# Narrowing in steps, products moved to GpSimd and ones products in the prologue of a two-block kernel

## The chip, the cores and the metric

The kernel runs on one core of one Trainium2 chip. The metric is the device time of one execution in microseconds, as the median over runs. The core has five engines with instruction queues of their own: TensorE (PE in the profile, its weight loads PEld) for matrix products, VectorE (DVE), ScalarE (ACT), GpSimd (POOL) and SyncE (SP), which here only issues transfers. Every queue is worked off in order. An instruction waits on semaphores for what it needs from other engines.

## The reference

Two blocks follow one another. The first is a linear attention over q, k, v of shape (4, 4, 1088, 32) (batch, heads, sequence, head dimension) with two random 8x32 matrices S1, S2 as sketches:

```python
def phi(x):
    a = np.einsum('rd,bhsd->bhsr', S1, x)
    b = np.einsum('rd,bhsd->bhsr', S2, x)
    return np.einsum('bhsi,bhsj->bhsij', a, b).reshape(*x.shape[:-1], r * r)
q_p, k_p = (phi(q), phi(k))
kv = np.einsum('bhsf,bhsd->bhfd', k_p, v)
z = np.sum(k_p, axis=2)
num = np.einsum('bhsf,bhfd->bhsd', q_p, kv)
den = np.einsum('bhsf,bhf->bhs', q_p, z)[..., None] + 1e-06
return (num / den).astype(np.float32)
```

Its result, laid out as x of 4352 tokens by 128, goes through a gated feed-forward block with 1536 hidden units:

```python
gate = 1.0 / (1.0 + np.exp(-(x @ w_gate)))
val = x @ w_val
return (gate * val @ w_out).astype(np.float32)
```

S1, S2 and the three weight matrices arrive as 64-bit floats, everything else as 32-bit floats.

## The kernel before

**The feed-forward block** holds tokens in chunks of 512 columns of `xT` (eight full ones and a half one) and hidden units in 12 blocks of 128. One *wave* (`w1`, L287) is one block for one chunk: the gate and the value product into the two halves of a PSUM tile (`wave`, L300, two products of 512 columns, which the profile counts as four records), the sigmoid on ScalarE (`sg`, L308), and later the product of both on VectorE (`g`, L313, by `glu`). `w2` (L252) adds g times w_out into `moeout` (L258), about two waves later, and after the twelfth block turns and stores the chunk. A *slot* (`slot`, L327) runs one group of attention work and then some waves, each with the `glu` of the wave before and a due `w2` ahead of it. So the attention of later batches is strewn between the waves, in an order that is written out by hand.

**Weights.** `load_w(n)` (L135) loads two blocks of all three matrices as pairs of 32-bit words into `w_in`, which has four buffers. `narrow` (L81) makes 32-bit floats from the halves: cap (L94, VectorE, clamps the upper word as a float), head (L99 and L103, VectorE, shifts and masks), tail (L107, ScalarE, the lower word), a Square of cap (L108, ScalarE), the add of tail to head as integers (L109, GpSimd), and at last the product into `w_sb` (L113, VectorE), which sets tiny values to zero. All but the last run at once in `narrow_w(j)` (L158), and the last in `narrow_last(j)` (L165). In chunk 0, wave j calls `narrow_w(j + 3)` and `narrow_last(j + 1)`; blocks 0, 1 and 2 are narrowed ahead of the first wave.

**Attention.** For a batch: `turn_k` (L351) and `turn_q` (L362) turn k and q on VectorE in blocks of 32; `kps` (L375) projects k with both sketches and turns the result into `kab`; `outer` (L395) makes the 64 features of k for one head as an outer product, on VectorE (L399, `kp`); `kv` (L450) sums features times v on TensorE (L459, `kvz`), and features times ones for z, or, in batches 1 to 3, z from `sum_z` (L489), four adds on VectorE (L493 to L497). `ab` (L406) projects q with the sketches spread over 64 columns (`aps`, `bps`, L422), copies one to SBUF on ScalarE (`asb`, L432) and multiplies on VectorE (`mult`, L441, `qp`). `ndt` (L500) turns the sums on TensorE and copies them on VectorE into `zb` (L514) and `nd` (L516). `den` (L518) gives the denominators, whose `invert` on VectorE (L534 to L541) makes `rb`, and `num` (L551) the numerators, whose `divide` (L568) writes `xT`. Queries go in two parts of 18 and 16 rows of 32 (`q_chk`).

**Order.** SP's queue first holds the loads of S1 and S2, batch 0's k and q, each in two parts, v, the weights 0 to 7 and batch 1. The prologue (L578 to L601) runs batch 0 up to the first part of xT, with the narrowing of blocks 0 and 1 between `kv` and `ndt`, and of block 2 after `divide`. Then come seven slots with one wave each, the loop over batches 1 to 3, in which batch 1 has one wave a slot and the others mostly two, and the remaining waves. PSUM tile `wave` has two buffers, shared by waves, `aps` and some `bps`; the tiles `two` (kps, bps, nps) and `one` (kvz, ndps, dps) have one each.

Of the kernel before, what the change touches and what calls it, by code (L numbers as in the profile page):

```python
# [20 lines left out]
def kernel(  # L21
# [34 lines left out]
    sbN = ctx.enter_context(tc.tile_pool(name="sbN", bufs=4))  # L56
# [17 lines left out]
    q_chk = [(0, 9), (9, TP - 9)]  # L74
# [6 lines left out]
    def narrow(out, bits):  # L81
# [7 lines left out]
        def tmp(dt, tag):  # L89
            return sbN.tile([P, 3, P], dt, tag=tag, name=tag)[:, :n, :m]  # L90


        cap, head, tail = tmp(I32, "cap"), tmp(I32, "head"), tmp(I32, "tail")
        nc.vector.tensor_scalar(  # L94
            out=cap.bitcast(F32), in0=hi.bitcast(F32), scalar1=122880.0, scalar2=-122880.0,
            op0=ALU.min, op1=ALU.max,
        )

        nc.vector.tensor_scalar(  # L99
# [6 lines left out]

        nc.scalar.activation(out=tail, in_=lo, func=ACTF.Copy, scale=2.0**-29)  # L107
        nc.scalar.activation(out=cap.bitcast(F32), in_=cap.bitcast(F32), func=ACTF.Square)  # L108
        nc.gpsimd.tensor_tensor(out=head, in0=head, in1=tail, op=ALU.add)  # L109


        def last():
            nc.vector.scalar_tensor_tensor(  # L113
                out=out, in0=cap.bitcast(F32), scalar=1.265625 * 2.0**-30, in1=head.bitcast(F32),
                op0=ALU.is_ge, op1=MUL,
            )

        return last
# [37 lines left out]
    narrowed = {}  # L156

    def narrow_w(j):  # L158
# [6 lines left out]
    def narrow_last(j):  # L165
        if j in narrowed:
            narrowed.pop(j)()


    def load_rows(src, b, tag, parts=((0, T),)):  # L170
        t = ld.tile([P, T, D], F32, tag=tag, name=tag)
        for t0, t1 in parts:
            nc.sync.dma_start(
# [24 lines left out]
    halves = ((0, T0), (T0, T))  # L198
# [16 lines left out]

    sig0 = const.tile([P, 1], F32, tag="sig0")
    nc.scalar.activation(out=sig0, in_=ones[:, :1], func=ACTF.Sigmoid)
    if wide:
        narrow(sr, sr_in)()
    ident = const.tile([P, P], F32, tag="ident")  # L220
    make_identity(nc, ident)

    hm = const.tile([P, 2, R], F32, tag="hm")
    nc.vector.memset(hm, 0.0)
    for h in range(H):
        nc.vector.memset(hm[32 * h : 32 * h + 32, h % 2, :], 1.0)

# [13 lines left out]

    zb = []
    for n in range(2):
# [43 lines left out]
    def w1():  # L287
# [399 lines left out]
```

## Time and profile before

| | |
|---|---|
| median of 3 runs | 342.51 us (342.16 to 343.34) |
| profiled execution, its own time | 344.44 us |
| its span, first to last instruction | 342.6 us |
| TensorE busy | 314.2 us, 92% |
| VectorE busy | 163.3 us, 48% |
| ScalarE busy | 85.1 us, 25% |
| GpSimd busy | 15.0 us, 4% |
| first wave starts | 24.90 us |

Times of a row are microseconds from the start of the span. A row of a group ends with the idle time of the engine just before these instructions, and what ended it. "x4" counts records; a 32-bit product is two records. TensorE's busy time also counts the slow parts, where the granted clock is half.

### The profile page before, as it was taken

To read this page: it belongs to the slowest core of one execution; us is meant where nothing else is said; L and a number is where in the kernel's file an instruction comes from. 1 tells how busy PE (TensorE), PEld (TensorE's weight loads), DVE (VectorE), ACT (ScalarE), POOL (GpSimd) and SP (SyncE) were. 2 spreads that over 40 slices of the span, in tenths; PEclk is the share of its full clock that TensorE was granted. 3 is DMA by queue.
4 is the path that set the end of the run, shared out by engine and by line. 5 is a ranking of instruction groups with operands and counts; after the bars stand their busy time and mean duration, and the time that the engine had idled before them with its cause. 6 is when DMAs were issued, how large, how long until landed. Compare 5 with 4: busy or idle time off the path is not lost.

```text
span 342.6 us, 3915 instructions
## 1 busy us (share of the span) xinstructions
PE 314.2 (92%) x1552; PEld 137.8 (40%) x1552; DVE 163.3 (48%) x294; ACT 85.1 (25%) x152; POOL 15.0 (4%) x21
## 2 busy tenths in 40 slices
PE   1839878599999999999999999999999999999994
PEld 0512323133334434334443344444444444444682
DVE  3874798965675455475344432233233232322321
ACT  2143442123122222222222122222222222222220
POOL 1032131110000000000000000000000000000000
PEclk9995999989999999999999999999999999999999
DMA  6999302211100001000100010002001000100010
GB/s 166 303 316 310 65 0 68 65 35 36 31 2 1 2 16 17 0 0 2 31 2 0 0 32 2 0 0 32 0 0 25 7 0 0 32 0 0 2 31 15
DMA packets 25586, 14.08 MB, mean 41 GB/s; under 512 B 19168, under 2 KB 22752, under 8 KB 25568
## 3 DMA queue, kind: packets, MB, share of 16 engines
q1 hardware_dynamic: 25568, 13.83, 16.0%
q8 instruction: 12, 0.20, 0.2%
q14 instruction: 6, 0.05, 0.0%
HBM read 11.60 MB, written 2.23 MB: 40 GB/s over the span
## 4 chain that ended last, share of the span: by engine, by line
PE 83%; DVE 10%; DMA 2%; issue 2%; ACT 1%; SPq 1%; DVEq 0%
PE wave L300 49%; PE moeout L258 25%; PE aps L422 3%; PE kvz L459 2%; DMA q<-in_q_dram 2%; DVE g L313 1%; PE dps L523 1%; DVE head L103 1%; DVE cap L94 1%; PE nps L558 1%; DVE w_sb L113 1%; PE bps L422 1%; DVE head L99 1%; DVE kp L399 1%; DVE qT L368 1%
## 5 line engine op out<-in xcount | busy, mean ns | idle before, releaser
L300 PE MATMUL wave<-xT,w_sb 128*128 128x512 f32 (+1 forms) x432 | 195.7, 581 | 6.0 <-DVE w_sb L113 4.8
L313 DVE TENSOR_TENSOR g<-wave,sg 128x512 f32<-128x512 f32 x102 | 69.9, 685 | 122.7 <-ACT sg L308 122.7
L300 PEld LDWEIGHTS wave<-xT,w_sb 128*128 128x128 f32 x432 | 82.3, 193 | 103.4 <-issue 84.1
L308 ACT ACTIVATE sg<-wave 128x512 f32<-128x512 f32 x102 | 60.8, 596 | 204.3 <-PE wave L300 204.3
L258 PE MATMUL moeout<-g,w_sb 128*128 128x512 f32 (+1 forms) x216 | 107.4, 590 | 1.8 <-DVE g L313 1.8
L258 PEld LDWEIGHTS moeout<-g,w_sb 128*128 128x128 f32 x216 | 38.1, 191 | 44.1 <-issue 38.0
L441 DVE TENSOR_TENSOR qp<-bps,asb 128x576 f32<-128x576 f32 (+1 forms) x16 | 11.4, 720 | 22.9 <-PE bps L422 17.9
L422 PE MATMUL aps<-qT,s 32*64 32x288 f32 (+1 forms) x128 | 12.4, 468 | 5.0 <-DVE qT L368 2.8
L109 POOL TENSOR_TENSOR head<-head,tail 128x384 int32<-128x384 int32 (+1 forms) x13 | 14.1, 1089 | 55.3 <-DVE head L103 42.4
L108 ACT ACTIVATE cap<-cap 128x384 f32<-128x384 f32 (+1 forms) x13 | 6.5, 502 | 29.4 <-DVE head L103 29.4
L380 PE MATMUL kps<-kT,sk 64*32 64x288 f32 x64 | 3.9, 482 | 9.6 <-DVE kT L356 9.6
L399 DVE TENSOR_TENSOR kp<-kab 128x576 f32<-128x576 f32 (+2 forms) x20 | 12.5, 665 | 0.0
L422 PE MATMUL bps<-qT,s 32*64 32x288 f32 (+1 forms) x128 | 12.2, 451 | 0.0
L432 ACT COPY asb<-aps 128x576 f32<-128x576 f32 (+1 forms) x16 | 9.8, 610 | 8.0 <-PE aps L422 6.5
L422 PEld LDWEIGHTS aps<-qT,s 32*64 32x64 f32 x128 | 4.0, 147 | 18.2 <-issue 9.1
L568 DVE TENSOR_TENSOR xT<-nps,rb 128x576 f32<-128x576 f32 (+1 forms) x8 | 5.8, 724 | 7.7 <-PE nps L558 7.6
L459 PE MATMUL kvz<-kp,v 128*32 128x64 f32 (+1 forms) x288 | 8.8, 246 | 0.2 <-DVE kp L399 0.2
L459 PEld LDWEIGHTS kvz<-kp,v 128*32 128x32 f32 (+1 forms) x288 | 6.3, 124 | 6.2 <-issue 4.0
L103 DVE SCALAR_TENSOR_TENSOR head<-cap,head 128x384 int32<-128x384 int32 (+1 forms) x13 | 6.9, 533 | 0.5
L368 DVE STREAM_TRANSPOSE qT<-q 128x576 f32<-128x576 f32 (+1 forms) x8 | 5.9, 736 | 1.7 <-DMA q<-in_q_dram 1.7
L268 DVE STREAM_TRANSPOSE o_sb<-moeout 128x512 f32<-128x512 f32 (+1 forms) x9 | 6.1, 676 | 1.2 <-PE moeout L258 1.2
L107 ACT ACTIVATE tail<-w_in 128x384 int32<-128x384 uint32 x12 | 6.6, 553 | 0.0
(46 smaller groups left out, 87.1 us busy)
## 6 DMA issues: line engine op xcount, KB each, us to landing
v<-in_v_dram SPq DMA_DIRECT2D x16, 144.0 KB, 7.6
k<-in_k_dram SPq DMA_DIRECT2D x3, 544.0 KB, 7.0
q<-in_q_dram SPq DMA_DIRECT2D x3, 544.0 KB, 8.5
w_in<-in_moe_w_gate_dram SPq DMA_DIRECT2D x6, 256.0 KB, 5.6
w_in<-in_moe_w_val_dram SPq DMA_DIRECT2D x6, 256.0 KB, 5.6
w_in<-in_moe_w_out_dram SPq DMA_DIRECT2D x6, 256.0 KB, 5.7
out_dram<-o_sb SPq DMA_DIRECT2D x20, 64.0 KB, 2.0
k<-in_k_dram SPq DMA_DIRECT2D x1, 288.0 KB, 2.9
```

The source lines that it names most:

```text
L103: nc.vector.scalar_tensor_tensor(out=head, in0=cap, scalar=-0x40000000, in1=head, op0=ALU.bitwise_and, op1=ALU.bitwise_or)
L109: nc.gpsimd.tensor_tensor(out=head, in0=head, in1=tail, op=ALU.add)
L258: nc.tensor.matmul(out=moe["acc"][:, :tw], lhsT=w_sb[:, 2, j, :], rhs=g[:, jj, :tw], start=(j == 0), stop=(j == NJ - 1),)
L300: nc.tensor.matmul(out=wv[:, which, jj * tw : (jj + 1) * tw], lhsT=w_sb[:, which, j0 + jj, :], rhs=xT[:, t0 : t0 + tw], start=True, stop=True,
L308: nc.scalar.activation(out=sg, in_=wv[:, 0], func=ACTF.Sigmoid)
L313: nc.vector.tensor_tensor(out=g, in0=wv[:, 1], in1=sg, op=MUL)
L368: nc.vector.transpose(out=qT_of[b][:, t0 : t0 + tn].rearrange("p t c s -> p (t c s)"), in_=q_t[b][:, 2 * t0 : 2 * (t0 + tn)].rearrange("p ...
L399: nc.vector.tensor_tensor(out=KP[b][:, h, j0:j1].rearrange("p j (i l) -> p j i l", i=R), in0=bass.AP(tensor=a0.tensor, offset=a0.offset, a ...
L422: nc.tensor.matmul(out=dst[64 * c : 64 * c + 64, m, : 32 * tn], lhsT=sx[rows, :], rhs=qT_of[bb][rows, t0 : t0 + tn, c, :], start=True, sto ...
L432: nc.scalar.copy(out=ASB[a_of][:, :, :w], in_=aps[:, :, :w])
L441: nc.vector.tensor_tensor(out=QP[bb][:, 2 * pr : 2 * pr + 2, 32 * t0 : 32 * t0 + w], in0=bps[:, :, :w], in1=ASB[b_of][:, :, :w], op=MUL,)
L459: nc.tensor.matmul(out=kvz[32 * h : 32 * h + 32, F * which : F * which + F], lhsT=v_t[b][:kr, h, j, :] if which == 0 else ones[:kr, :], rh ...
```

## The change

- **Loads:** the first part of batch 0's k (18 rows of 32) is issued on ScalarE's queue, ahead of all else there; q's first part has 16 rows instead of 18, and its second part is loaded after the first weights.
- **Ones products:** `warm(n)` issues n products of a constant 128x128 view of ones with itself, into a buffer of `wave` that nothing reads: 14 at the start, 4 after `kps(0)`, 4 after the first `ab` groups.
- **Small moves in the prologue:** the constants hm, ident and zb are made before S1 and S2 are narrowed.
- **Narrowing in three steps:** `narrow` becomes a generator. Step 0 is cap, for the weights now on GpSimd, and tail; step 1 is head, Square and add; step 2 the last product. In chunk 0, wave j runs step 0 of block j + 4, step 1 of j + 2 and step 2 of j + 1. Ahead of the first wave stand step 0 of blocks 0 to 3, steps 1 of blocks 0 and 1 and step 2 of block 0.
- **GpSimd:** `outer` runs there for all batches, except for three of four heads in batch 0, and so do the four adds of `sum_z`.
- **ScalarE:** makes the copy into `nd`.
- **Slots:** the prologue's slots become nine, with `turn_k(1)` a slot ahead of `kps(1)`, and `outer` of batch 1 between slots. In the loop, `kv` runs in one slot for all nine steps, later than before; the `ab` groups of a batch follow one another; batch 1 has one wave a slot, the others two.

```diff
-    q_chk = [(0, 9), (9, TP - 9)]
+    q_chk = [(0, 8), (8, TP - 8)]
...
+        cap, tail = tmp(I32, "cap", 5), tmp(I32, "tail", 4)
+        eng.tensor_scalar(
             out=cap.bitcast(F32), in0=hi.bitcast(F32), scalar1=122880.0, scalar2=-122880.0,
             op0=ALU.min, op1=ALU.max,
         )
-
+        nc.scalar.activation(out=tail, in_=lo, func=ACTF.Copy, scale=2.0**-29)
+        yield
+
+        head = tmp(I32, "head", 3)
         nc.vector.tensor_scalar(
...
         nc.gpsimd.tensor_tensor(out=head, in0=head, in1=tail, op=ALU.add)
...
+        yield
+
+        nc.vector.scalar_tensor_tensor(
+            out=out, in0=cap.bitcast(F32), scalar=1.265625 * 2.0**-30, in1=head.bitcast(F32),
+            op0=ALU.is_ge, op1=MUL,
+        )
+        yield
...
+    def narrow_w(j, step):
+        if not 0 <= j < NJ:
+            return
         n, jj = divmod(j, 2)
         if wide:
-            narrowed[j] = narrow(w_sb[:, :, j, :], w_in[n][:, :, jj])
-        if jj == 1 and n + 4 < NJ // 2:
+            if step == 0:
+                narrowing[j] = narrow(w_sb[:, :, j, :], w_in[n][:, :, jj], nc.gpsimd)
+            next(narrowing[j])
+        if step == 0 and jj == 1 and n + 4 < NJ // 2:
             load_w(n + 4)
...
-    k_t[0] = load_rows(k, 0, "k", halves)
-    q_t[0] = load_rows(q, 0, "q", halves)
+    k_t[0] = load_rows(k, 0, "k", ((0, KBASE[2] + 1, nc.scalar), (KBASE[2] + 1, T, nc.sync)))
+    q_t[0] = load_rows(q, 0, "q", ((0, T0, nc.sync),))
     v_t[0] = load_v(0)
-    for n in range(4):
+    load_w(0)
+    load_rows(q, 0, "q", ((T0, T, nc.sync),), q_t[0])
+    for n in range(1, 4):
         load_w(n)
...
+    def warm(n):
+        t = psm.tile([P, 2, 512], F32, tag="wave", name="warm")
+        x = bass.AP(tensor=ones.tensor, offset=ones.offset, ap=[list(ones.ap[0]), [0, P]])
+        for _ in range(n):
+            nc.tensor.matmul(out=t[:, 0, :P], lhsT=x, rhs=x, start=True, stop=True)
+
+    warm(14)
...
-            if j0 + 3 < NJ:
-                narrow_w(j0 + 3)
-            narrow_last(j0 + 1)
+            narrow_w(j0 + 4, 0)
+            narrow_w(j0 + 2, 1)
+            narrow_w(j0 + 1, 2)
...
-    def outer(b, h, j0=0, j1=NJK):
+    def outer(b, h, j0=0, j1=NJK, eng=nc.gpsimd):
...
-        nc.vector.tensor_copy(out=ND[b], in_=ndps[:, 0, :P])
+        nc.scalar.copy(out=ND[b], in_=ndps[:, 0, :P])
...
     kps(0)
+    warm(4)
     ab((0, 0, 0))
     mult00 = ab((0, 1, 0), (0, 0, 0))
     mult10 = ab(None, (0, 1, 0), (psm, "wave"))
-    for h in range(H):
-        outer(0, h, 0, 5)
-    kv(0, [1, 2, 3, 4])
-    for h in range(H):
-        outer(0, h, 5, NJK)
+    warm(4)
+    for j0, j1 in ((0, 5), (5, NJK)):
+        outer(0, 3, j0, j1)
+        for h in range(3):
+            outer(0, h, j0, j1, nc.vector)
+        if j0 == 0:
+            kv(0, [1, 2, 3, 4])
     mult00()
     mult10()
     kv(0, [5, 6, 7, 8, 0])
-    narrow_w(0)
-    narrow_w(1)
+    narrow_w(0, 0)
+    narrow_w(1, 0)
+    narrow_w(0, 1)
     ndt(0)
+    narrow_w(2, 0)
+    narrow_w(3, 0)
     invert = den(0, 0)
     divide = num(0, 0)
     invert()
     divide()
-    narrow_w(2)
-    narrow_last(0)
+    narrow_w(0, 2)
+    narrow_w(1, 1)
     turn_q(0, 1)
...
     slot(lambda: r_group((0, 1, 1), (0, 0, 1)), 1)
-    turn_q(1, 0)
-    slot(lambda: r_group((1, 0, 0), (0, 1, 1)), 1)
+    slot(lambda: r_group(None, (0, 1, 1)), 1)
     slot(lambda: den(0, 1)(), 1)
     slot(lambda: num(0, 1)(), 1)
     turn_k(1)
+    slot(None, 1)
     slot(lambda: kps(1), 1)
+    turn_q(1, 0)
+    outer(1, 0)
+    slot(lambda: r_group((1, 0, 0), None), 1)
+    outer(1, 1)
...
+        slot(lambda: r_group((b, 1, 0), (b, 0, 0)), wn)
         if b == 1:
+            outer(b, 2)
+        turn_q(b, 1)
+        slot(lambda: r_group((b, 0, 1), (b, 1, 0)), wn)
+        if b == 1:
+            outer(b, 3)
+        zs = sum_z(b)
+        slot(lambda: r_group((b, 1, 1), (b, 0, 1)), wn)
+        turn_k(b + 1)
+        slot(lambda: kv(b, [1, 2, 3, 4, 5, 6, 7, 8, 0], zs), wn)
+        if more:
+            slot(lambda: kps(b + 1), wn)
             for h in range(H):
-                outer(b, h)
...
+                outer(b + 1, h)
         turn_q(b + 1, 0)
...
+        slot(lambda: ndt(b), wn)
+        slot(lambda: r_group((b + 1, 0, 0) if more else None, (b, 1, 1)), wn)
+        slot(lambda: den(b, 0)(), wn)
...
-        slot(num0_den1, 1)
-        if more:
-            outer(b + 1, 3)
+        slot(num0_den1, wn)
         slot(lambda: num(b, 1)(), 1)
```

More of the change, by code (lines that the diff above doesn't have):

```diff
@@ L226 @@
         nc.vector.memset(hm[32 * h : 32 * h + 32, h % 2, :], 1.0)
+    ident = const.tile([P, P], F32, tag="ident")
+    make_identity(nc, ident)
+    zb = []
+    for n in range(2):
+        t = const.tile([P, H, 32], F32, tag=f"zb{n}", name=f"zb{n}")
+        nc.gpsimd.memset(t, 0.0)
+        zb.append(t)
+    if wide:
+        for _ in narrow(sr, sr_in, nc.vector):
+            pass
     sk = const.tile([P, 2, 2, R], F32, tag="sk")
@@ L240 @@
     sk = sk.rearrange("p m n r -> p (m n r)")
-    zb = []
-    for n in range(2):
-        t = const.tile([P, H, 32], F32, tag=f"zb{n}", name=f"zb{n}")
-        nc.gpsimd.memset(t, 0.0)
-        zb.append(t)
     xT = const.tile([P, NTOK], F32, tag="xT")
@@ L398, in outer @@
         jn = j1 - j0
-        nc.vector.tensor_tensor(
+        eng.tensor_tensor(
             out=KP[b][:, h, j0:j1].rearrange("p j (i l) -> p j i l", i=R),
@@ L576, in num, with r_group @@
         return divide
-    turn_k(0, halves)
+    def r_group(a_of, b_of):
+        m = ab(a_of, b_of)
+        if m is not None:
+            m()
+    turn_k(0, ((0, KBASE[2] + 1), (KBASE[2] + 1, T)))
     turn_q(0, 0)
     kps(0)
+    warm(4)
     ab((0, 0, 0))
```

69 lines of the change are left out of this document (15 added, 54 removed).

## The prediction

> **What bounds the kernel now.** I read the page's head and its row of granted clock by slices first, then stretches cut where the granted clock changes. Columns of the second fence: stretch, its length, busy time of PE, PEld, DVE, ACT and POOL with instruction counts, granted clock, DMA share, GB/s.
>
> ```profile
> span 342.6 us, 3915 instructions
> PEclk9995999989999999999999999999999999999999
> ```
>
> ```profile
> 20.80:24.20 3.40, 0.05 (x8) 0.00 (x0) 3.16 (x7) 0.00 (x0) 0.00 (x0) 1.00 1.06 274
> ...
> 31.05:34.50 3.45, 3.45 (x12) 1.00 (x18) 0.90 (x2) 0.76 (x2) 1.18 (x1) 0.50 1.02 317
> 34.50:68.60 34.10, 25.56 (x179) 8.93 (x163) 30.80 (x54) 11.31 (x23) 7.09 (x6) 1.00 0.18 49
> 65.20:68.60 3.40, 1.21 (x19) 0.25 (x17) 3.26 (x7) 0.00 (x0) 0.00 (x0) 1.00 0.00 0
> 68.60:72.00 3.40, 3.19 (x8) 1.09 (x5) 3.37 (x7) 1.48 (x3) 1.18 (x1) 0.50 0.00 0
> 80.00:337.00 257.00, 256.49 (x1056) 114.63 (x1054) 103.10 (x171) 59.97 (x101) 0.00 (x0) 1.00 0.05 9
> ```
>
> From 80 us on TensorE does not stop (256.49 of 257 us), and the change takes no product away from it. So only what lies before 80 us can be won. There VectorE is the bound from 34.5 to 68.6 (30.80 of 34.10 us, TensorE idle 8.5), and TensorE has half its clock twice: after it stood still from 20.8 to 24.2, until 34.5, and again after a stretch with 1.21 us of work. VectorE's groups from 24.9 to 72 us (busy us, mean ns):
>
> ```profile
> L313 DVE TENSOR_TENSOR g<-wave,sg 128x512 f32<-128x512 f32 x9 | 6.1, 676 | 2.0 <-ACT sg L308 2.0
> L113 DVE SCALAR_TENSOR_TENSOR w_sb<-cap,head 128x384 f32<-128x384 f32 x10 | 5.5, 552 | 0.0
> L103 DVE SCALAR_TENSOR_TENSOR head<-cap,head 128x384 int32<-128x384 int32 x9 | 5.0, 559 | 0.3
> L94 DVE TENSOR_SCALAR cap<-w_in 128x384 f32<-128x384 f32 x9 | 4.8, 534 | 0.0
> L399 DVE TENSOR_TENSOR kp<-kab 128x576 f32<-128x576 f32 x4 | 3.6, 948 | 0.0
> L99 DVE TENSOR_SCALAR head<-cap 128x384 int32<-128x384 int32 x9 | 3.2, 360 | 0.3
> L441 DVE TENSOR_TENSOR qp<-bps,asb 128x512 f32<-128x512 f32 (+1 forms) x4 | 2.8, 711 | 4.2 <-PE bps L422 3.2 <-PE aps L422 1.0
> L356 DVE STREAM_TRANSPOSE kT<-k 128x1088 f32<-128x1088 f32 x2 | 2.6, 1302 | 0.0
> ```
>
> The change takes the caps (4.8), the outer products (3.6) and batch 1's sums off this list. The way to the first wave, from the timeline (start, length, idle before and its releaser), the key/value products in the chain of waits, and their record means of 0 to 17.4 us and of 100 to 320 us:
>
> ```profile
> 9.32 0.78 DVE L368 STREAM_TRANSPOSE qT<-q 128x576 f32<-128x576 f32 x1 [1.67 <-DMA q<-in_q_dram]
> 10.02 0.81 DVE L390 STREAM_TRANSPOSE kab<-kps 128x288 f32<-128x288 f32 x2
> 10.75 3.00 DVE L399 TENSOR_TENSOR kp<-kab 128x320 f32<-128x320 f32 x8
> 15.27 0.55 DVE L94 TENSOR_SCALAR cap<-w_in 128x384 f32<-128x384 f32 x1 [0.19 <-DMA w_in<-in_moe_w_out_dram]
> 17.69 0.37 ACT L482 COPY kvd<-kvz 128x256 f32<-128x256 f32 x1 [4.54 <-PE kvz L459]
> 18.20 0.41 PE L503 MATMUL ndps<-ident,kvd 128*128 128x128 f32 x2 [0.59 <-ACT kvd L482]
> 19.07 0.29 DVE L516 COPY nd<-ndps 128x128 f32<-128x128 f32 x1
> 20.26 0.48 DVE L534 STREAM_TRANSPOSE dT<-dps 128x288 f32<-128x288 f32 x1 [0.90 <-PE dps L523]
> 22.17 0.76 DVE L568 TENSOR_TENSOR xT<-nps,rb 128x576 f32<-128x576 f32 x1
> 24.90 3.78 PE L300 MATMUL wave<-xT,w_sb 128*128 128x512 f32 x4 [4.05 <-DVE w_sb L113]
> ```
>
> ```profile
> 13.46 4.20 PE kvz L459 x144
> ```
>
> ```profile
> L459 PE MATMUL kvz<-kp,v 128*32 128x64 f32 x64 | 3.4, 314 | 0.0
> ```
>
> ```profile
> L459 PE MATMUL kvz<-kp,v 128*32 128x64 f32 (+1 forms) x144 | 3.1, 223 | 0.0
> ```
>
> A key/value record takes 314 ns early against 223 later: TensorE starts at half clock, though the early clock rows say otherwise. Between xT (22.17 + 0.76) and the first wave (24.90) stand the first three operations of narrowing block 2 and the last of block 0, 1.97 us.
>
> **The change, part by part.** *Prices on GpSimd.* First the lock, in timeline rows and in the minimum, median and maximum of two lines, ns:
>
> ```profile
> 42.96 1.18 POOL L109 TENSOR_TENSOR head<-head,tail 128x384 int32<-128x384 int32 x1 [3.71 <-DVE head L103]
> 43.77 0.41 DVE L536 TENSOR_SCALAR rc<-dT 128x16 f32<-128x16 f32 x1
> ```
>
> ```profile
> L536 DVE TENSOR_SCALAR rc<-dT x8: 172/174/411, 20.8 to 191.1; 128x18 f32<-128x18 f32 x4, 128x16 f32<-128x16 f32 x4
> ```
>
> ```profile
> L493 DVE TENSOR_TENSOR z<-kp x3: 1214/1217/2023, 63.6 to 153.9; 128x1024 f32<-128x1024 f32 x3
> ```
>
> ```profile
> 5.10 0.29 POOL masks.py:199 TENSOR_SCALAR_AFFINE_SELECT ident<-ident 128x128 f32<-128x128 f32 x1
> ...
> 18.60 1.96 POOL L109 TENSOR_TENSOR head<-head,tail 128x384 int32<-128x384 int32 x2 [12.92 <-ACT tail L107]
> ```
>
> L536 needs 174 ns and took 411 at 43.77, ending at 44.18 as GpSimd's add ended at 44.14; L493 needs 1.22 us and took 2.02 at 63.6 beside another add. So some VectorE operations stand still while GpSimd works, and each operation moved there is paid in part by VectorE. The Trainium skill (SBUF — State Buffer, SBUF: two separate sides) says the two share one port pair, held for a whole instruction; the trace agrees by those 0.24 and 0.81 us. Its rule speaks against this change; by it two heads of outer products in parallel cost their sum.
>
> A two-input add of 384 costs 0.98 (1.96 for two), or 1.18 beside VectorE: 2.6 to 3.1 ns an element. An outer product of 576 is then 1.5 to 1.8 us; batch 1's sums (1024, 512, 256 and 256 elements) 5.2 to 6.3. A cap on GpSimd has no row; it has one tensor input: between 0.29 (128 elements, as if all fixed) and 1.18; I take 0.7, three times 0.29 less some fixed part. GpSimd's order is one queue; up to the key/value products of batch 1 it holds 12 caps, 12 adds, 6 outer products and the sums: 8.4 + 14.2 + 8.4 + 5.5 = 36.5 us from about 9.5, so done near 50 to 55, before the 13th wave that needs it (67, below).
>
> *Prologue.* The first part of k goes by ScalarE's queue past the loads of S on SP's, and q's second part moves behind the first weights. That issue stands ahead of ScalarE's table load, for which nothing waits so early. The loads of w4 and w5 wait on SP for the caps and tails that free their buffers; behind them stand only batch 2's, wanted tens of us later. VectorE's wait of 1.67 us for q can go wholly or not at all; I take 1.2: kab at 8.8, outer products from 9.5. Eight on VectorE took 3.00; six are 2.25, the two others 1.7 on GpSimd: together 2.25 if they overlap, 3.95 if they take turns; by the lock rows I take 3.7: done at 13.2. TensorE comes out of its 14 products warm; ten of the eighteen key/value steps are left then, of 4.20 us at half clock, so 10/18 of 2.1 = 1.2: kvd at 14.5 instead of 17.69. Behind it VectorE has the two mult (0.71 each, to 14.6) and now the two head steps of w0 (0.36 + 0.56, 0.3 of lock) ahead of the zb copies; so zb ends near 16.2, where it ended at 19.07, and dT starts at 17.1. dT to the end of xT is 2.67 (20.26 to 22.93); with 0.25 of lock at rc, 20.0 less what full clock saves of den, 0.2. Then only w_sb's product is left, 0.55, where before came 1.97: **first wave at 20.3 instead of 24.9**. Bounds 18.3 (no lock, full 1.67) and 22 (no gain at q; w0 no earlier than its 15.27). nd's copy moves to ScalarE, behind the Square of w0, which waits for these heads too: ready near 16.5, before num asks for it.
>
> *The 22 ones products.* 14 products are 28 records of 128 columns. A 512-wide record streams in 0.43 (1.72 for four, below), so 0.107 at full and 0.215 at half clock: 6.0 us, from about 1 to 7, some 2 us ahead of kab. The transposes, 128 wide, took 0.41 for two with all latency, which would make 5.7, and at half clock 11.5: the upper end. I take 6.0. The two groups of 4 fall into waits for q and the outer products; uncovered they cost at most 0.9 each.
>
> *The clock afterwards.* From num to the first wave TensorE again idles some 3.1 us. The row of 65.20 shows that 1.21 us of work in 3.4 already lost the clock, so half clock comes again. It came back only after a stretch without a pause (31.05 to 34.50): in the new order wave 2 starts 5.5 after wave 1 (below), and a filled stretch ends 3.4 to 6.8 later, near 31. By the Trainium skill (TensorE: Matmul & The Clock Gate, What's actually happening) half clock follows at least one idle window of about 3.4 us; 3.1 us would hold none, the first rival. The trace differs: the stretch of 65.20 was not idle.
>
> *The slots of chunk 0.* From the chain of waits:
>
> ```profile
> 30.44 3.78 PE wave L300 x4
> ...
> 73.41 0.83 PE kvz L459 x40
> ...
> 75.55 1.72 PE wave L300 x4
> 77.88 1.06 PE moeout L258 x2
> 78.94 1.72 PE wave L300 x4
> ```
>
> TensorE needs 1.72 for a wave, half of it (0.86, two records of four) for moeout, and for a group of eight or sixteen products 0.3 to 0.6 (75.55 + 1.72 = 77.27 to 77.88): 2.6 to 3.2 us. VectorE needs 0.68 (g) + 0.36 + 0.56 + 0.55 = 2.15 without the cap, plus the group: den 1.91 (20.26 to 22.17), num and turn_k 0.7 + 1.3, kps 0.81 and turn_q 0.78, the slot with mult and turn_q 0.71 + 0.78. The longer of the two, starting from 20.3: wave 2 at 25.8 (as 24.90 to 30.44), wave 3, after 3.4 for wave 2 and 1.3 and 1.7 for group and moeout at half clock (the last of it at full), at 31.8; then 3.0, 4.2, 4.3, 2.7, 3.9, 3.0, 3.9, 3.4, 3.4: the 12th wave at 63.6. I add 1.2 of lock in the slots that VectorE binds: 64.8, against 78.94. Bounds of this lock: none, and 11 (three waits of 0.3 in each of 12 narrowings).
>
> **Sum.** At the 12th wave the old order had the key/value products (0.83) behind it, the new one not: 78.94 - 64.8 - 0.83 = 13.3 us. Span 342.6 - 13.3 = 329.3. The profiled execution took 344.44 with its launch, its span is 0.1 over the runs' median of 342.51; so the forecast is **329 us**. In the later batches the moved operations cost nothing, since TensorE binds there and VectorE has 154 of 257 us free; uncovered, an outer product late by 1 us costs 1 us only if kv meets it.
>
> **Rivals.**
> - *The clock stays full, or is back after one wave.* For it: the gap is 3.1 us, under the 4.05 of before. Against: the 65.20 row. Waves 2 to 4 come 6 us earlier: 323.
> - *VectorE and GpSimd take turns.* For it: the rows of L536 and L493; GpSimd would be busy over half of the stretch. 7 of the 11 us show, the rest lies in TensorE's half clock: 336.
> - *The prologue does not move.* The ones products hold TensorE until 12.4 (11.5 us), or w0's arrival stays where it was; first wave near 24.9: 334.
> - *Slower than before: GpSimd's queue is late for batch 1's key/value products*, and all waves stand behind these on TensorE. Its 36.5 us may grow by some 15 before anything waits; with operations twice my price it ends at 9.5 + 73 = 82.5, 15.5 past 67: 345. It decides from a factor 1.9 on. Against: the adds' rows.
> - *No effect that shows*: gains and lock cancel, 342.5.
>
> **How the numbers follow.** Forecast 0.50, full clock 0.18, turns 0.17, prologue 0.08, GpSimd late 0.04, no effect 0.03. About 0.3% is what a measurement of this kernel can tell from no change. Faster 0.93, same 0.03, slower 0.04. The forecast's own range, by a first wave at 18.3 to 22 and 0 to 4 us of lock, is 325 to 334; 321 to 337 takes in most of the first three rivals.
>
> **What would show it.** First wave near 20; TensorE's granted clock half from about 20 to 31 and never again; no wait of TensorE for L94's successor; key/value products early at 223 ns a record; GpSimd busy some 55 to 60 us, VectorE some 25 less; L103, L113 or L536 lengthened where GpSimd works; the 12th wave near 65. A first wave after 23, or key/value products of batch 1 waiting for GpSimd, would make me wrong.

## The result and the profile after

The changed kernel takes **333.05 us** (median of four runs, 333.0 to 333.84), beside 342.34 us for the kernel before on the same chip: a ratio of 0.974 with a 95% interval of 0.969 to 0.979. The forecast was 329 with a range of 321 to 337: the time lies inside the range, 4 us above the forecast. The profiled execution took 333.0 us, its span is 331.2, 11.4 less than before; the forecast's span was 329.3. That the span fits to 1.9 us is luck: it comes from two large misses of opposite sign, as the stages show. Some executions have a lower granted clock and take longer; times and ratios here leave these out, but the profile of the kernel with the outer products and sums of batches 1 to 3 back on VectorE is of such an execution.

First the page's head of the changed kernel, then three of its stretches (columns as in the prediction: length, busy time of PE, PEld, DVE, ACT, POOL, granted clock, DMA share, GB/s). Line numbers are those of the changed kernel.

```profile
span 331.2 us, 4024 instructions
PE 313.7 (95%) x1596; PEld 141.8 (43%) x1596; DVE 140.9 (43%) x252; ACT 86.3 (26%) x156; POOL 52.3 (16%) x59
PEclk9967999999999999999999999999999999999998
```

```profile
14.83:18.24 3.41, 0.42 (x21) 0.22 (x10) 0.94 (x3) 0.00 (x0) 0.00 (x0) 1.00 1.07 379
25.12:65.36 40.24, 37.84 (x193) 13.72 (x193) 31.65 (x60) 18.91 (x36) 23.78 (x24) 0.96 0.32 99
106.00:186.00 80.00, 79.27 (x458) 33.46 (x457) 30.90 (x54) 19.24 (x34) 9.71 (x8) 1.00 0.04 7
```

From the first wave (25.12) to the twelfth (65.36), TensorE is busy 37.84 of 40.24 us: it is the bound there now, where VectorE was before. The clock falls once, after the first stretch shown, in which TensorE does almost nothing, and not again before the last product. The way to the first wave, in the timeline of each engine:

```profile
4.80 0.20 DVE L95 TENSOR_SCALAR cap<-sr_in 128x64 f32<-128x64 f32 x1 [3.45 <-DMA sr_in<-in_S_dram]
9.09 0.85 DVE L401 STREAM_TRANSPOSE kab<-kps 128x288 f32<-128x288 f32 x2 [0.22 <-PE kps L391]
9.86 3.89 DVE L410 TENSOR_TENSOR kp<-kab 128x320 f32<-128x320 f32 x6
20.21 0.34 DVE L525 COPY zb<-ndps 64x4 f32<-64x4 f32 x2 [4.40 <-PE ndps L514]
23.91 0.69 DVE L579 TENSOR_TENSOR xT<-nps,rb 128x512 f32<-128x512 f32 x1
```

```profile
18.36 0.33 PE L470 MATMUL kvz<-kp,v 64*32 64x64 f32 x4 [3.11 <-issue]
...
25.12 3.65 PE L311 MATMUL wave<-xT,w_sb 128*128 128x512 f32 x4 [2.05 <-DVE w_sb L114]
...
65.36 1.93 PE L311 MATMUL wave<-xT,w_sb 128*128 128x512 f32 x4
```

The outer products end at 9.86 + 3.89 = 13.75. TensorE runs the key/value products right behind them at full clock, and then stands still for 3.11 us with nearly all of them done. The profile names no releaser: "issue" means that TensorE waited for nothing it can show. Most of VectorE's idle time before zb (4.40) hangs on this; in the first kernel below, without the pause, it is 1.22. The first wave starts at 25.12, where before it was 24.90 and the forecast 20.3. TensorE's waits from 8 to 70 us (total, times, longest):

```profile
PE kvz L470 <- issue: 3.1, 1, 3.1
PE wave L311 <- DVE w_sb L114: 2.0, 1, 2.0
...
PE aps L433 <- DVE qT L379: 1.6, 2, 0.9
...
PE wave L311 <- ACT asb L443: 0.8, 1, 0.8
```

In the slots `turn_q` is late twice, and wave 2 waits once for ScalarE's `asb`. GpSimd's groups from 9 to 70 us and two of VectorE's from 25 to 66:

```profile
L111 POOL TENSOR_TENSOR head<-head,tail 128x384 int32<-128x384 int32 x12 | 13.5, 1126 | 26.4 <-DVE head L107 19.5 <-ACT tail L99 6.8
L95 POOL TENSOR_SCALAR cap<-w_in 128x384 f32<-128x384 f32 x12 | 6.8, 573 | 0.0
L410 POOL TENSOR_TENSOR kp<-kab 128x576 f32<-128x576 f32 x4 | 4.6, 1170 | 0.0
L504 POOL TENSOR_TENSOR z<-kp 128x1024 f32<-128x1024 f32 x1 | 2.6, 2615 | 0.1
```

```profile
L107 DVE SCALAR_TENSOR_TENSOR head<-cap,head 128x384 int32<-128x384 int32 x11 | 6.3, 577 | 0.4
L103 DVE TENSOR_SCALAR head<-cap 128x384 int32<-128x384 int32 x11 | 4.9, 442 | 0.0
```

### The profile page after: what moved, and what is told of

Read it like the earlier page. It is cut to its first block, busy times and chain, and to the rows that moved or that the text cites. A ratio compares the mean times of both kernels' runs of the same rounds, so it can differ in the third digit from the quotient of the medians.

```text
span 331.2 us, 4024 instructions
## 1 busy us (share of the span) xinstructions
PE 313.7 (95%) x1596; PEld 141.8 (43%) x1596; DVE 140.9 (43%) x252; ACT 86.3 (26%) x156; POOL 52.3 (16%) x59
## 4 chain that ended last, share of the span: by engine, by line
PE 88%; DVE 7%; issue 2%; ACT 1%; DMA 1%; SPq 0%; POOL 0%; DVEq 0%; ACTq 0%; POOLq 0%
PE wave L311 51%; PE moeout L269 27%; PE aps L433 3%; PE kvz L470 2%; PE dps L534 2%; PE nps L569 1%; DVE g L324 1%; PE bps L433 1%; DMA sr_in<-in_S_dram 1%; DVE head L107 1%; DVE w_sb L114 1%; PE kps L391 1%; PE warm L223 1%; DVE kT L367 1%; ACT asb L443 1%
## 5 line engine op out<-in xcount | busy, mean ns | idle before, releaser
L311 PE MATMUL wave<-xT,w_sb 128*128 128x512 f32 (+1 forms) x432 | 193.1, 574 | 3.5 <-DVE w_sb L114 2.0
L410 POOL TENSOR_TENSOR kp<-kab 128x576 f32<-128x576 f32 (+2 forms) x14 | 15.5, 1132 | 43.1 <-DVE kab L401 43.1
L452 DVE TENSOR_TENSOR qp<-bps,asb 128x512 f32<-128x512 f32 (+1 forms) x16 | 11.5, 723 | 23.3 <-PE bps L433 17.7
L111 POOL TENSOR_TENSOR head<-head,tail 128x384 int32<-128x384 int32 (+1 forms) x13 | 13.8, 1064 | 30.4 <-DVE head L107 23.6
L433 PE MATMUL aps<-qT,s 32*64 32x256 f32 (+1 forms) x128 | 10.8, 413 | 1.6 <-DVE qT L379 1.6
L433 PE MATMUL bps<-qT,s 32*64 32x256 f32 (+1 forms) x128 | 11.2, 411 | 0.3 <-ACT asb L443 0.3
L443 ACT COPY asb<-aps 128x512 f32<-128x512 f32 (+1 forms) x16 | 9.7, 612 | 6.6 <-PE aps L433 5.5
L579 DVE TENSOR_TENSOR xT<-nps,rb 128x512 f32<-128x512 f32 (+1 forms) x8 | 5.8, 724 | 10.6 <-PE nps L569 10.5
L223 PE MATMUL warm<-ones 128*128 128x128 f32 x44 | 7.4, 336 | 1.0 <-DVE hm L230 1.0
L223 PEld LDWEIGHTS warm<-ones 128*128 128x128 f32 x44 | 6.9, 245 | 1.8 <-DVE hm L230 0.9
L504 POOL TENSOR_TENSOR z<-kp 128x1024 f32<-128x1024 f32 x3 | 7.5, 2484 | 0.2
```

What stands on the lines that cost most here:

```text
L223: nc.tensor.matmul(out=t[:, 0, :P], lhsT=x, rhs=x, start=True, stop=True)
L311: nc.tensor.matmul(out=wv[:, which, jj * tw : (jj + 1) * tw], lhsT=w_sb[:, which, j0 + jj, :], rhs=xT[:, t0 : t0 + tw], start=True, stop=True,
L410: eng.tensor_tensor(out=KP[b][:, h, j0:j1].rearrange("p j (i l) -> p j i l", i=R), in0=bass.AP(tensor=a0.tensor, offset=a0.offset, ap=[pst ...
L433: nc.tensor.matmul(out=dst[64 * c : 64 * c + 64, m, : 32 * tn], lhsT=sx[rows, :], rhs=qT_of[bb][rows, t0 : t0 + tn, c, :], start=True, sto ...
L443: nc.scalar.copy(out=ASB[a_of][:, :, :w], in_=aps[:, :, :w])
L452: nc.vector.tensor_tensor(out=QP[bb][:, 2 * pr : 2 * pr + 2, 32 * t0 : 32 * t0 + w], in0=bps[:, :, :w], in1=ASB[b_of][:, :, :w], op=MUL,)
```

## The experiments

The question that stood first was the pause of 3.11 us. Theory: TensorE had no instructions. The trace lists transfers of 16 KB on a queue of their own ("q8 instruction"), twelve over the span, and the first in the span begins at 15.90 and lasts 1.05 us, inside the pause. TensorE had by then used up what it held. Rivals: the pause belongs to the key/value products' data, or to a time. The page's row (packets, MB, share of 16 engines):

```profile
q8 instruction: 12, 0.20, 0.2%
```

**Without the ones products.**

```diff
-    warm(14)
...
-    warm(4)
...
-    warm(4)
```

> The changed kernel without its 22 ones products. In the changed kernel TensorE stopped in the midst of batch 0's key/value products from 15.25 to 18.36 us, with no releaser ('issue'). Theory F (fetch): it had run out of instructions; the next 16 KB packet of them came at 15.90 to 16.95, late among the data transfers, and the 88 instructions of the ones products had eaten the stock. Then the pause goes (under 0.5 us), key/value records go back to about 314 ns, the first wave starts near 23.5 to 24, and the time is 331.5 to 333. Theory W (a wait that belongs to this place of the program; before the change there was a pause of 0.17 us at the same place): the pause of 3 us stays, everything in front is slower by half clock, first wave after 26, time 335.

329.85 us (328.54 to 331.91), ratio 0.9675 [0.9621, 0.9729], span 328.6. The key/value products have no pause; the first wave starts at 22.23, 2.9 us earlier. The ratio's interval overlaps that of the changed kernel, so how much of this reaches the total is open; the first wave is the firmer figure. The warm TensorE does win something: without the ones kab comes at 9.57 instead of 9.09, and a key/value record takes 313 ns instead of 220 (first this kernel, then the changed one). The pause costs more: kvd starts at 16.64 here and at 19.06 there.

```profile
L469 PE MATMUL kvz<-kp,v 128*32 128x64 f32 x64 | 3.5, 313 | 0.0
```

```profile
L470 PE MATMUL kvz<-kp,v 128*32 128x64 f32 x64 | 1.9, 220 | 0.0
```

**The same time in fewer instructions:** six products of 512 columns (4, 1, 1) instead of 22 of 128.

```diff
+        xw = bass.AP(tensor=ones.tensor, offset=ones.offset, ap=[list(ones.ap[0]), [0, 512]])
...
-            nc.tensor.matmul(out=t[:, 0, :P], lhsT=x, rhs=x, start=True, stop=True)
+            nc.tensor.matmul(out=t[:, 0, :], lhsT=x, rhs=xw, start=True, stop=True)
...
-    warm(14)
+    warm(4)
...
-    warm(4)
+    warm(1)
...
-    warm(4)
+    warm(1)
```

> The changed kernel with 6 ones products of 512 columns (4, 1 and 1) in place of 22 of 128: about the same TensorE time and clock, 64 instructions fewer. Theory F: the pause of 3.1 us shrinks to under 1 us or moves to the products of num, key/value records stay at 223 ns, the first wave starts near 22.5, the time is 330 to 331.5. Theory W: pause and time as they are, 333.0, first wave 25.1.

329.59 us (329.29 to 330.27), ratio 0.9665 [0.9626, 0.9703]. The pause moves out of the key/value products into the numerators and shrinks to 1.1. Counting TensorE's records from the start up to the pause, products and weight loads together, shows why. First the changed kernel, then this one, each with its row of waits or its stretch:

```profile
0.00:15.25 15.25, 12.35 (x221) 9.95 (x222) 9.89 (x28) 3.56 (x8) 4.42 (x13) 1.00 0.86 270
```

```profile
0.00:18.00 18.00, 14.71 (x221) 6.56 (x222) 11.23 (x32) 6.30 (x15) 6.22 (x16) 1.00 0.92 290
```

```profile
PE nps L570 <- issue: 1.1, 1, 1.1
```

221 + 222 = 443 records in both, though other products stand there. The pause is bound to a count of instructions. With fewer instructions the ones products bring the first wave to 21.46, 0.8 us ahead of the kernel without them although 1.1 of pause is left; in the total the two, 329.59 and 329.85, can't be told apart.

**k's first part back on SP's queue.**

```diff
-    k_t[0] = load_rows(k, 0, "k", ((0, KBASE[2] + 1, nc.scalar), (KBASE[2] + 1, T, nc.sync)))
+    k_t[0] = load_rows(k, 0, "k", ((0, KBASE[2] + 1, nc.sync), (KBASE[2] + 1, T, nc.sync)))
```

> The changed kernel with batch 0's first part of k back on SP's queue, behind S1 and S2. S landed 1.0 us later with k beside it (3.1 us after its issue, 2.1 before the change); I expect it back at 2.1, VectorE's first narrowing at 3.7 instead of 4.80, kT at about 6.0 instead of 6.92, and q's first part near 8.6, so that qT waits some 0.4 us. By theory F the time does not follow, since TensorE's restart at 18.36 hangs on the fetch: 332.5 to 333.3. If instead the chain through S, kT and kab sets the first wave, it comes 0.5 earlier: 332.5.

333.95 us (333.87 to 334.61), ratio 0.9789 [0.9744, 0.9834], not to be told from the changed kernel. S is in SBUF at 3.80 instead of 4.80 and all of the prologue comes 1.0 us earlier up to the pause, which is 3.4 us and again at 443 records. The first wave gains only 0.7 (24.39); and the half clock, which lasts to 33.53 here against 28.5, takes it back in wave 2. So S was held up by k, whose transfer on ScalarE's queue began beside it.

**Batch 0's outer products all on VectorE again.**

```diff
-        outer(0, 3, j0, j1)
-        for h in range(3):
+        for h in range(H):
             outer(0, h, j0, j1, nc.vector)
```

> The changed kernel with all four heads' outer products of batch 0 on VectorE again (the later batches' stay on GpSimd). If VectorE and GpSimd take turns at a port, eight on VectorE take 3.0 us where six beside GpSimd's two took 3.89, so the products of mult start 0.9 us earlier; if they overlap, it takes 0.75 longer than 2.25, so 3.0 too, but then the 3.89 is not explained. The time: by theory F none of it shows, 333.0; if the outer products are on the way to the first wave, 332.1.

334.36 us (333.51 to 335.18), ratio 0.9801 [0.9756, 0.9847], not to be told from the changed kernel. All eight take 3.66 us, beside GpSimd's first two caps; the six of the changed kernel took 3.89, beside two outer products (1.72) and the same caps (1.42) on GpSimd. With GpSimd idle eight took 3.00 in the kernel before, so six would take 2.25: VectorE lost 1.64 us to GpSimd's 3.14. The two engines held each other up for about half of that time, and the prologue's offload is worth nothing.

```profile
9.97 3.66 DVE L410 TENSOR_TENSOR kp<-kab 128x320 f32<-128x320 f32 x8
```

**Caps on VectorE again**, and, in another kernel, **the outer products and sums of batches 1 to 3 there again.**

```diff
-                narrowing[j] = narrow(w_sb[:, :, j, :], w_in[n][:, :, jj], nc.gpsimd)
+                narrowing[j] = narrow(w_sb[:, :, j, :], w_in[n][:, :, jj], nc.vector)
```

```diff
-    def outer(b, h, j0=0, j1=NJK, eng=nc.gpsimd):
+    def outer(b, h, j0=0, j1=NJK, eng=nc.vector):
...
-        nc.gpsimd.tensor_tensor(out=z4, in0=kp[:, :, 1:5], in1=kp[:, :, 5:9], op=ALU.add)
+        nc.vector.tensor_tensor(out=z4, in0=kp[:, :, 1:5], in1=kp[:, :, 5:9], op=ALU.add)
```

> The changed kernel with the 12 caps of the weights on VectorE again, all else as it is. Way to the first wave: hidden behind the pause of TensorE, so first wave 25.1 to 25.6. In the slots VectorE needs 2.7 us and the group instead of 2.15; if VectorE binds there, as I forecast for the slots of den, num, kps and of mult with turn_q, the 12 waves take 2 to 3 us longer than the 40.2 of the changed kernel and the time is 335 to 336. If TensorE binds all slots with room to spare, nothing: 333.

> The changed kernel with the outer products of batches 1 to 3 and the four adds of sum_z on VectorE again. VectorE then has 4 x 0.74 and 2.75 us more between the 8th and the 12th wave. If VectorE binds there: 1.5 to 4 us more, 334.5 to 337. If the room that the moved caps and the new order leave is enough: 333.

336.72 us (335.49 to 338.18), ratio 0.9834 [0.974, 0.9928], and 339.15 (337.33 to 340.61), ratio 0.9897 [0.9851, 0.9943]. From the first wave to the twelfth the two profiles take 43.6 and 45.6 us instead of 40.2; the second is of an execution of 342.80 us, so its 45.6 is too much for that kernel. The first kernel's stretch, the part of it at half clock, and its wait for `turn_q`; then the same of the second, with its wait after the twelfth wave:

```profile
25.36:68.96 43.60, 39.99 (x192) 13.92 (x193) 34.62 (x68) 18.94 (x36) 19.70 (x16) 0.92 0.29 87
55.87:59.28 3.41, 3.41 (x5) 1.03 (x4) 1.17 (x3) 0.53 (x2) 2.28 (x2) 0.50 0.00 0
```

```profile
PE aps L433 <- DVE qT L379: 2.6, 2, 1.8
```

```profile
25.17:70.79 45.62, 41.74 (x193) 14.97 (x193) 37.90 (x67) 18.82 (x36) 16.62 (x19) 0.87 0.28 83
```

```profile
PE aps L433 <- DVE qT L379: 3.1, 2, 2.3
...
PE aps L433 <- DVE g L324: 1.7, 1, 1.7
```

With caps on VectorE it is late by little (1.0 us more for qT), and that costs a clock: 3.41 us at half clock lose about 1.7, and TensorE idles 1.2 us longer (43.60 - 39.99 against 40.24 - 37.84), together 2.9 of the 3.4. With both offloads in place TensorE is fed well enough to hold the clock, in these profiles. But the loss doesn't need the clock. The fastest execution of the first kernel, 335.49, has a mean granted clock of 0.985, above the 0.981 of the changed kernel's profile, and is still 2.4 us longer than the changed kernel's median; the fastest of the second, 337.33, has 0.981 and is 4.3 longer. There the late VectorE itself costs that much.

No run takes back the narrowing in three steps or the new order of the slots alone, so what these are worth stays open.

**Is the packet late because of the data transfers?** Three kernels held loads back behind qp (near 14.9 us), by a small transfer on SP that reads it; in the first two all weights from the third set on, or from the second, with batch 1's loads; the third of these combines the hold with the wide ones and k on SP.

```diff
-    for n in range(1, 4):
-        load_w(n)
...
-    load_batch(1)
...
     mult10()
+    gate = const.tile([P, 1], F32, tag="gate", name="gate")
+    nc.sync.dma_start(out=gate, in_=QP[0][:, 2, :1])
+    for n in range(1, 4):
+        load_w(n)
+    load_batch(1)
```

> The changed kernel, 22 ones products and all, but the loads of the weights 4 to 7 and of batch 1 held on SP's queue until the product of batch 0's mult is made (a small transfer that reads it stands ahead of them), so that few data transfers are under way when TensorE asks for its next 16 KB of instructions, near its 170th row at 12 us. Theory F with the data transfers as the cause of the delay: the packet comes within 1.5 us of 12, the pause after row 449 is under 0.5 us, first wave near 22, time 329.5 to 331. If instructions come late for another reason (the fetch takes 4 us whatever else runs): packet near 16, pause about 3 us, time 333.

> The changed kernel, but all weights behind the first set and batch 1's loads are issued only after the small transfer that reads qp (near 14.9 us), so that the DMA engines run dry near 11 us. If the 16 KB instruction packet of TensorE, asked for near 12 us, is late because it queues behind data transfers, it comes by 14 us here, the pause at row 449 (3.1 us in the changed kernel) is gone, and the first wave comes near 22, unless the second weight set, which now lands near 18, holds it up: 330 to 331. If the packet is late for another reason (its request comes late, or its latency is fixed), it comes at 15.3 to 16.9 again, a pause of 1.5 us or more stays, and the time is 332.5 to 334.

> The changed kernel with 6 ones products of 512 columns, k's first part on SP's queue and the loads held back as above. By theory F no pause is left (the run with wide ones alone still had 1.09 us at row 449), S lands 1.0 us earlier, first wave near 20 to 20.5 against 21.4 with wide ones alone; 327.5 to 329.5. If held loads cost elsewhere (w2 late for its cap, batch 1 late), first wave or later waves wait and it is 330 or more.

The first two give 332.70 us (ratio 0.9709 [0.9646, 0.9772]) and 334.17 (0.9743 [0.9671, 0.9815]). They did not test the theory, since the order in which the kernel's instructions are queued is not that of its text: SP's queue still had two more weight sets ahead of the gate, and DMA engines stayed full until about 15.4 (the second kernel; its last transfer ahead of the gate and the gate in SP's timeline, then its DMA engines from 10 to 18 us in slices of 0.2, in tenths).

```profile
10.54 0.38 SPq L151 DMA_DIRECT2D w_in<-in_moe_w_out_dram  x1
14.90 0.54 SPq L608 DMA_DIRECT2D gate<-qp  x1
```

```profile
DMA  9698899999999999999999999865002105647979
```

The packet came at 15.52, as the engines ran dry, and the pause was 2.9. I took this at first for the opposite finding, a block that needs its 5 us whatever else moves, and tested both with the next two kernels. The combined kernel gives 329.25 (0.9616 [0.9554, 0.9679]), first wave at 20.36, pause 1.1.

**More instructions, and a hold that holds.** In one kernel the first 14 products become 8 of 128 and 70 of 32 columns. In the other the weights from the second set on and batch 1's loads wait for small ScalarE copies of qp into their buffers, which no order can pass.

```diff
-    def warm(n):
+    def warm(n, c=P):
...
-    warm(14)
+    warm(8)
+    warm(70, 32)
```

```diff
             w_in[n] = raw.tile([P, 3, 2, P, 2], I32, tag="w_in", name="w_in")
+            if 1 <= n < 4:
+                nc.scalar.copy(out=w_in[n][:, :, 0, 0, 0].bitcast(F32), in_=QP[0][:, 2, :3])
...
     mult10()
+    for n in range(1, 4):
+        load_w(n)
+    load_batch(1)
```

> The changed kernel, but the first 14 products of ones become 8 of 128 columns and 70 of 32 columns: 128 rows of TensorE more, in about the same time. If TensorE's instructions come in blocks of 256 rows, and the next block is ready some 5.3 us after TensorE has passed into the last one it has (row 193 at 13.09 and row 450 at 18.36 in the changed kernel), then row 193 is passed near 10 instead of 13.1, row 449 falls into the key/value products near 14, and the pause is about 1.3 us instead of 3.1: first wave near 23.3, 331 to 332, faster than the changed kernel although TensorE has more to do. If the pause is bound to the key/value products, to a time, or to the transfers then under way, it stays near 3: 333 or more.

> The changed kernel with the weights behind the first set and batch 1's loads held until qp is written (near 14.9 us) by small ScalarE copies into their buffers, so that the loads cannot move ahead as they did in the two softer holds; the DMA engines run dry near 11 us. If data transfers delay TensorE's packet, it starts before 14.6 and the pause falls below 1.5 us: first wave near 23.5, unless the second weight set, now landing near 18 to 19, is late for it: 331 to 332. If a block takes its 5 us whatever else moves, the pause stays between 2.8 and 3.4 with idle DMA engines, and the time is 333 to 335.

The first takes 333.46 us (333.36 to 335.72), ratio 0.9732 [0.9669, 0.9795]. My count was wrong: a product is two records on PE and two on PEld, so 64 more products are 256 records, a whole block, and the pause (2.5 us) stands at the same products, one block later:

```profile
0.00:16.50 16.50, 15.02 (x349) 12.98 (x350) 10.11 (x29) 3.56 (x8) 4.25 (x13) 1.00 0.88 275
```

349 + 350 = 699 = 443 + 256. The instruction queue also carries one transfer of 16 KB more, 13 instead of 12, so it is TensorE's. The miss settles the size of the block better than the test that was meant.

```profile
q8 instruction: 13, 0.21, 0.3%
```

The second takes **330.11 us** (329.81 to 330.62), ratio 0.9623 [0.9558, 0.9689]. The DMA engines in the same window, from 10 to 18 us, first in the changed kernel and then in this one, and this one's wait and first wave:

```profile
DMA  9999999999999999999999999999999999999999
```

```profile
DMA  9999852000000300000000000000994599999898
```

```profile
PE kvz L473 <- issue: 0.6, 1, 0.6
```

```profile
21.61 3.78 PE L314 MATMUL wave<-xT,w_sb 128*128 128x512 f32 x4 [2.62 <-DVE w_sb L114]
```

The lone 3 near 12.7 is the packet, on one of sixteen idle engines (this row counts a transfer's whole time where it starts). It begins 0.06 us after TensorE has started on the last 256 records that it holds; in the others it begins 2.1 to 3.6 us after. Worked out from the start times of TensorE's records and the transfer records:

```text
kernel                 last 256 begun   packet begins   pause
changed                     13.09           15.90        3.1
wide ones                   12.95           16.53        1.1
k on SP                     12.09           14.94        3.4
outers on VectorE           13.20           16.15        3.3
hold, second                13.02           15.52        2.9
256 records more            14.08           16.18        2.5
hold that holds             12.61           12.67        0.6
no ones products            13.67           16.87       none (used up at 24.1)
```

So the packet waits its turn among the data transfers, and the pause is gone but for 0.6 us when there are none, with the ones products still there. The theory of a fixed delay of 5 us falls. A part of it stays fixed: from the packet's end to TensorE's next record it is 1.4 to 1.6 us in all kernels of this table that pause.

**No ones products and k on SP.**

> The changed kernel without the 22 products of ones and with the first part of k back on SP's queue. S lands near 3.8 instead of 4.8, TensorE takes fewer than 449 rows before its packet, so there is no pause; everything from kab on comes 1 us earlier than without the ones alone: first wave near 21.3, 328.9. If the clock's stretches fall badly, as in the changed kernel with k on SP, where wave 2 was cold too, 330 to 332.

328.57 us (327.97 to 329.18), ratio 0.9605 [0.9552, 0.9657], the shortest time measured and faster than both kernels. It is the changed kernel with both edits shown above, and its first wave comes when the forecast had it. Its key/value records take 221 ns, as warm as with the ones: the trace's clock records begin at full clock at 10.04 us here, and only at 16.06 in the other kernel without ones. Why TensorE was warm so early here no run shows.

```profile
19.97 2.92 PE L310 MATMUL wave<-xT,w_sb 128*128 128x512 f32 x3 [2.04 <-DVE w_sb L114]
```

## Why the prediction was right in its range and wrong in two terms

The span came out 1.9 us over the forecast's 329.3: the first wave 4.8 later (25.12 for 20.3), the twelve waves 4.3 shorter (40.2 for 44.5), and the stages behind them 1.35 longer (from the twelfth wave to the end 265.84 us against 263.66, less the key/value products of 0.83 that the forecast had moved there). That the first two nearly cancel is luck.

The time is 4.05 us over the forecast of 329. The other 2.1 us are in the last step of the sum, "its span is 0.1 over the runs' median of 342.51; so the forecast is 329 us". A time is longer than its span (333.0 and 331.2 here, 344.44 and 342.6 before), and the span before came out at the median of the times only because the profiled execution was about 2 us slower than that median. A span of 329.3 means a time near 331. By the medians the change gained 9.3 us, and the forecast was 13.5.

**The prologue: the step that failed.** It is "ten of the eighteen key/value steps are left then ... so 10/18 of 2.1 = 1.2: kvd at 14.5". Half of it was right: TensorE came out warm, and the products ran at 220 ns a record. But I priced the ones products by the time they take and not by the instructions they are: 88 records of the 443 that TensorE had before it needed a block that was still waiting behind loads. kvd came at 19.06. A first wave after 23 was the prediction's own sign that would make it wrong, and it came at 25.12. Without the pause (no ones, k on SP) kvd starts at 14.38, within 0.12 of the forecast, and the first wave at 19.97. Part of this agreement is chance: the outer products end at 12.82 there, before the forecast's 13.2, and TensorE was warm without the ones to which the forecast gave the merit.

```profile
19.06 0.37 ACT L493 COPY kvd<-kvz 128x256 f32<-128x256 f32 x1 [7.22 <-PE kvz L470]
```

```profile
14.38 0.37 ACT L492 COPY kvd<-kvz 128x256 f32<-128x256 f32 x1 [3.33 <-PE kvz L469]
```

The Trainium skill (Runtime: NRT & Kernel Launch, Instruction fetch mechanics) says that instructions are refilled in blocks of 16 KiB, 256 of them, by the engine's own transfers while it works, and that crossing a block is mostly hidden. The runs agree on the size (443 and 699) and not on the hiding. The last 256 before the pause were used up in 15.04 - 13.09 = 1.95 us, while the next ones could start only at 18.36, 5.3 us after 13.09: 2.8 until the packet began, 1.05 for it, and 1.4 more.

The rival "the prologue does not move" (334, 0.08) had the outcome and not the cause: the ones products ended at 6.07, as forecast, and w0 was in time. I had forecast 13.2 for the end of the outer products with turns between the engines, and 13.75 was measured, in part by chance: the caps beside the outer products, which the forecast did not count there, took their share (six took 3.23 us, not 3.89, with k on SP, where the caps began only at 11.82); kab was 9.09 for 8.8, because S came 1.0 later, which I had not seen: "The first part of k goes by ScalarE's queue past the loads of S" was read as a gain for k and a cost for nobody.

**The clock.** Half clock "from about 20 to 31 and never again" was 18.25 to 28.5, and never again. It came 2 us earlier, with the pause, and ended ahead of wave 2 (30.16), which the forecast had cold. The rival of a clock that stays full falls in this order of work: even without the pause, with 1.91 us of work in the 3.41 before, it dropped at 16.86 (no ones, k on SP). In the combined kernel it held over a stretch with 1.84 and dropped after one with 1.36 (stretches, busy times and clock as before; first the kernel without ones, then two of the combined one):

```profile
13.45:16.86 3.41, 1.91 (x67) 1.01 (x58) 1.71 (x5) 2.48 (x7) 1.57 (x3) 1.00 1.07 373
```

```profile
16.06:19.47 3.41, 1.84 (x24) 0.47 (x24) 1.91 (x5) 0.96 (x3) 1.14 (x3) 1.00 1.03 354
...
22.89:26.30 3.41, 1.36 (x7) 0.68 (x4) 2.71 (x6) 2.24 (x5) 1.78 (x4) 1.00 1.06 223
```

So what decides isn't the busy time of a stretch alone; the limit stays open.

**The slots: the right mechanism, mis-sized.** VectorE stopped being the bound, as forecast. Of the 4.3 us by which the twelve waves were shorter, 2.9 are the clock's: wave 2 came 5.04 after wave 1 and wave 3 3.55 after wave 2, where 5.5 and 6.0 were forecast. Another 1.2 is the lock that was added. The nine slots behind took 31.65 together, against 31.8 without lock, but only because two errors cancel. "The longer of the two" in each slot was too strict: the slots of den and num were put at 4.2 and 4.3 with VectorE's work, and took 3.39 and 3.42, TensorE's; VectorE, with 31.65 of 40.24 us busy, spreads such a slot over its neighbours. Against that came `turn_q`'s wait, 1.6 us in two slots, which I had not named: they were put at 3.0 and 3.4 and took 4.28 and 4.31. Lock between the engines is there: L103 of the narrowing takes 442 ns on average, where before it was 360. That is 0.9 us over eleven; but the ones right ahead of the two late `turn_q` took 0.34 and 0.35, so these waits don't come from it. By the rule of the lock the rival of turns had 336; the stretch ends on TensorE instead.

**GpSimd's prices.** The outer product of 576 took 1.17 us, under my 1.5 to 1.8; the sums 2.62 + 1.28 + 0.73 + 0.73 = 5.4, at the low end; the cap 0.57 for 0.7. GpSimd is busy 52.3 (forecast 55 to 60), VectorE 22.4 less (forecast 25). No products of batch 1 waited for GpSimd, so the rival of 345 did not come, but by a small margin. The forecast had GpSimd's queue done "near 50 to 55"; its last sum ended at 68.33, and TensorE's first product with the sums started at 68.49:

```profile
67.60 0.73 POOL L508 TENSOR_TENSOR zs<-zs,kp 64x256 f32<-64x256 f32 x1
```

```profile
68.49 0.32 PE L482 MATMUL kvz<-zs,ones 128*32 128x64 f32 x8
```

The forecast added up GpSimd's work and left out its waits: its adds waited 19.5 us for VectorE's heads (the row of L111 above). Outer products and sums on VectorE again cost 6.1 us by the medians, 5.3 by the ratios; caps 3.7 or 3.1, with intervals of the ratios that overlap, so that for them the 3.4 us of the stretch of twelve waves is the firmer figure.

**The later batches** were put at nothing and cost 1.35: 0.73 is a wait of TensorE (79.27 of 80 us in the stretch shown), the rest is a term counted too small. Batch 1's key/value products, 80 records, now all lie behind the twelfth wave and take 1.52 (67.22 to the next moeout at 68.74); the 0.83 of the forecast were 40 of them, though the first 32 had run before the twelfth wave too in the old order (at 59.50).

## What to carry to other kernels

A filler that is meant to keep an engine warm is paid in instructions as well as in time: count the records on the engine up to its next block, and see whether the stretch there is one of many small products and whether the DMA engines are full. The shortest kernel here has no filler at all. A wait whose releaser is "issue" with a 16 KB instruction transfer inside it is that. And before reading a null result as a refutation, look whether the edit took effect: two holds here held too little, and the last settled it.

## What the hardware showed that I had not expected

- TensorE can use up 256 records in 1.95 us (key/value products of 64 columns). The next 256 were ready after 5.3 us among full DMA engines, and after 2.8 (12.61 to 15.40) with these idle, so a pause of 0.6 was left even there.
- A load of 64 KB (S) is delayed by 1.0 us when another queue starts a transfer of 288 KB beside it.
- Waits that grow by 1.0 us on TensorE in a phase that is nearly full can cost 1.7 more through the clock (caps on VectorE).
- VectorE and GpSimd hold each other up, but not for all of the time that both work: by the estimate above VectorE lost 1.64 us to 3.14 of GpSimd in the prologue.
